# Three moving operands of a sliding-window attention and gated feed-forward kernel are stored in reverse and read with a step of minus one

## Chip, cores and metric

The kernel runs on one core of one Trainium2 chip, in one launch. The time is device microseconds of that core, the median of several executions: 691.52 us before (three runs, 691.29 to 691.58). In the profile PE is the matmul engine and PEld its weight loads, DVE the vector engine, ACT the scalar engine, POOL the general one, SP the engine that issues most DMAs.

## What is computed

Attention over 4 batches x 8 heads, 768 positions, head size 64; each position sees a window of 128 positions and 4 sink positions. Then a feed-forward layer on 3072 tokens, 512 to 2048 to 512, with the gate `h - tanh(h)`:

```python
scores = scale * np.matmul(q, k.transpose(0, 1, 3, 2))
scores = np.where(is_sink | in_window, scores, -1000000000.0)
a = softmax(scores)                       # over keys
attn_out = np.matmul(a, v)
x = attn_out.transpose(0, 2, 1, 3).reshape(B * S, H * D)
h = x @ w_in
out = (h - np.tanh(h)) @ w_out
```

All data are float32 but for the feed-forward weights, which arrive as 64-bit words and are decoded on DVE.

## The kernel before

The work is cut into 12 chunks of 256 positions (`CH`), each with four units of two heads. Per unit: scores (`products`, L484 or L491), a mask and row maximum on DVE (L503, L509), exponentials on ACT (L517), normalisation (L538, L543), transposes of the probabilities on PE (L570), and masked copies of them into `pts` (L577, L584). Per chunk or pair of units, `attend` multiplies by the values (L618 for the sinks, L624 for the window) and leaves x, transposed, in PSUM.

Most matmuls are **split**: a float32 operand is written as a high part, rounded to the type `float32r`, and a low part that is the rest. A product takes two or three matmuls over such parts, in place of one plain float32 matmul. An operand's high part is written by an ACT copy and its low part by a DVE subtraction:

- keys of a unit: `ks`, one row of 392 keys for each of two heads, high and low parts in the two halves of the partitions (L448, L453). The first twelve units use plain float32 scores (L484) straight from the loaded keys and don't have `ks`; the other 36 take L491, four matmuls of 260 columns for each of the two 128-query tiles
- x of a chunk: `xh` and `xl`, 4 rows of 256 positions (L636, L640)
- weights: eight groups g for each of the two weight matrices k. `wt[k, g]` holds high and low part (L671, L676). For k = 0 (first weights) it is viewed as 4 rows of 256, for k = 1 (second weights) as 2 rows of 512

A step n of the feed-forward layer treats one chunk and one group. `mm1` (L695): 24 matmuls of 256 columns into `hps`, where the first weights are the stationary operand and xh or xl the **moving** one. `gate`: tanh on ACT (L700), a difference on DVE (L703), high part gh on ACT (L707), low part gl on DVE (L711). `mm2` (L743): 12 matmuls of 512 columns into `ops`, where gh or gl is stationary and the second weights are **moving**. There are 96 steps, so 2304 matmuls at L695 and 1152 at L743. After a chunk's last group the sums are copied (L754) and stored.

All engines' programs are written in an order that a planner works out beforehand: every piece of work is added with an engine, a duration, a due time and the tiles that it reads and writes, and `order` simulates the engines and picks the due piece that can start. The score matmuls, the transposes and the products with the values are placed among the feed-forward matmuls in that way. The durations and due times are constants in the code.

Of the kernel before, what the change touches and what calls it, by code (L numbers as in the profile page):

```python
# [9 lines left out]
F32 = mybir.dt.float32  # L10
F32R = mybir.dt.float32r
# [3 lines left out]
ALU = mybir.AluOpType  # L15
# [3 lines left out]
P = 128  # L19
DM = H * D  # L20
DFF = 2048
NPAIR = H // 2
# [4 lines left out]
KW = WIN + TS  # L27
KPACK = P + NT * TS
CH = 2 * P
# [123 lines left out]
def _words(t):  # L153

    w = t.rearrange("p (n w) -> p n w", w=2)
    return w[:, :, 0], w[:, :, 1]


def _decode_part(nc, m, lo, hi, i):


    if i == 0:
        nc.vector.tensor_scalar(m, hi, 3, 0x3FFFFFF8, op0=ALU.logical_shift_left, op1=ALU.bitwise_and)
    elif i == 1:
        nc.vector.scalar_tensor_tensor(m, lo, 29, m, op0=ALU.logical_shift_right, op1=ALU.bitwise_or)  # L165
    else:
        nc.vector.scalar_tensor_tensor(m, hi, 0xC0000000, m, op0=ALU.bitwise_and, op1=ALU.bitwise_or)  # L167


def _decode(nc, m, t):  # L170
    lo, hi = (w.bitcast(U32) for w in _words(t))
    for i in range(3):
        _decode_part(nc, m.bitcast(U32), lo, hi, i)


class Work:
# [63 lines left out]
def _banded(tc, qd, kp, vp, vs, masks, w_in, w_out, ident, pts, early, out):  # L240
    nc = tc.nc
    et = mybir.EngineType
    with ExitStack() as ctx:
# [193 lines left out]
        qh, ql, ks, pr, st, xps, xh, xl, sps, tps = ({} for _ in range(10))  # L437

        def split(u):

            def k_high(h):
                if h == 0:
                    t = hpool.tile([P, NPAIR * CH], F32R, tag="ha", name=f"ks{u}")
                    ks[u] = t[:, : 2 * KW].rearrange("p (h k) -> p h k", h=2)
                r = slice(64 * h, 64 * h + 64)
                nc.scalar.copy(ks[u][r, h, :], kt[u][r, :])  # L448

            def k_low(h):  # L450
                k, t = ks[u], kt[u]
                r, o = slice(64 * h, 64 * h + 64), slice(64 * (1 - h), 64 * (1 - h) + 64)
                nc.vector.tensor_tensor(k[o, h, :], t[r, :], k[r, h, :].bitcast(F32), op=ALU.subtract)  # L453

            def q_high():
                t = hpool.tile([P, 2, 2, CH], F32R, tag="hb", name=f"q{u}")
                qh[u], ql[u] = t[:, 0], t[:, 1]
                nc.scalar.copy(qh[u], qt[u])  # L458

            def q_low():  # L460
                nc.vector.tensor_tensor(ql[u], qt[u], qh[u].bitcast(F32), op=ALU.subtract)

            t = due_unit(u) - 5000
            k, q = ([s] for s in slots(u))
            old = [("x", 2)] + [("xu", 2, i) for i in range(NPAIR)] if u == 3 * NPAIR else []
            work.add("ACT", 525, t, q_high, q, ["qh"] + old)
            work.add("DVE", 705, t, q_low, q + ["qh"], ["ql"], port=True)
            for h in range(2):
                work.add("ACT", 425, t, lambda h=h: k_high(h), k, [("ks", h)] + old)
                work.add("DVE", 590, t, lambda h=h: k_low(h), k, [("ks", h)], port=True)  # L470
# [122 lines left out]
        def attend(cc, p0, pairs):  # L593

            b, c = chunks[cc]
            key, banks = (cc, p0), range(pairs // 2)

            def sink_rows():
                xps[key] = [ps_x.tile([P, 2, CH], F32, tag="x", name=f"x{cc}_{p0}")]
                for t in range(2):  # L600
                    nc.tensor.transpose(  # L601
                        xps[key][0][:, 1, t * P : (t + 1) * P],
                        zt[:, t].bitcast(F32).rearrange("p n a b c -> p (n a b c)"), ident,
                    )

            def sink_copy(m):

                nc.scalar.activation(zr[:, m, :], xps[key][0][:, 1, :], AF.Copy, scale=odd[:, m : m + 1])

            def values():  # L610
                if pairs == NPAIR:
                    ps = ps_t.tile([P, 2, 2, P], F32, tag="t", name=f"x{cc}_2")
                    xps[key].append(ps.rearrange("p a b q -> p a (b q)"))
                plan = [(2 * c, 0, CH, 1), (2 * c + 1, P, CH, 3)]
                if c > 0:
                    plan.append((2 * c - 1, 0, P, 0))
                for i in banks:
                    nc.tensor.matmul(xps[key][i], lhsT=vsink[:, p0 // 2 + i], rhs=zr, start=True, stop=False)  # L618
                for p in range(p0, p0 + pairs):
                    for n, (i, a, z, blk) in enumerate(plan):  # L620
                        for h in range(2):
                            rhs = pts[:, place(NPAIR * cc + p), h].rearrange("p a b -> p (a b)")[:, blk * P : blk * P + z - a]
                            hd = (2 * p + h) * D
                            nc.tensor.matmul(  # L624
                                xps[key][(p - p0) // 2][h * 64 : h * 64 + 64, p % 2, a:z],
                                lhsT=vt[cc, i][:, hd : hd + D], rhs=rhs,
                                start=False, stop=p % 2 == 1 and n == len(plan) - 1,
                            )

            def x_high(i):  # L630
                if p0 == 0 and i == 0:
                    where, a, b = (hpool, "hb", "ha") if home(cc) == 2 else (xpool, "xh", "xl")
                    xh[cc] = where.tile([P, NPAIR, CH], F32R, tag=a, name=f"xh{cc}")
                    xl[cc] = where.tile([P, NPAIR, CH], F32R, tag=b, name=f"xl{cc}")
                r = slice(p0 + 2 * i, p0 + 2 * i + 2)
                nc.scalar.copy(xh[cc][:, r, :], xps[key][i])  # L636

            def x_low(i):
                r = slice(p0 + 2 * i, p0 + 2 * i + 2)
                nc.vector.tensor_tensor(xl[cc][:, r, :], xps[key][i], xh[cc][:, r, :].bitcast(F32), op=ALU.subtract)  # L640

            last = NPAIR * cc + p0 + pairs - 1
            d = due_unit(last) + 5500
            work.add("PE", 230, d + 1500, sink_rows, [("z", i) for i in range(NPAIR)], ["x"])
            for m in range(2):
                work.add("ACT", 270, d + 2000, lambda m=m: sink_copy(m), ["x"], [("zr", m)])
            v = [vslot[cc, i] for i in range(max(0, 2 * c - 1), 2 * c + 2)]
            pt = [(f"pt {k}", place(NPAIR * cc + i)) for k in ("whole", "own", "before") for i in range(p0, p0 + pairs)]
            need = pt + ["vsink", ("zr", 0), ("zr", 1)] + v
            work.add("PE", (340 + 735 * pairs if c == 0 else 200 + TK * pairs), d + 3500, values, need, ["x", "t"][: pairs // 2])  # L650
            for i in banks:
                x = [("xu", home(cc), p0 + 2 * i), ("xu", home(cc), p0 + 2 * i + 1)]
                work.add("ACT", 490, d + 5000, lambda i=i: x_high(i), ["xt"[i]], x + [("x", home(cc))] * (p0 + i == 0))
                work.add("DVE", 690, d + 5200, lambda i=i: x_low(i), ["xt"[i]], x)


        wm, wt = {}, {}

        def weights(k, g):
            key, r = (k, g), count[0] % 2  # L660
            count[0] += 1

            wm[key] = pts[:, 2 + r].rearrange("p h a b -> p (h a b)")

            def bits(i):
                lo, hi = (w.bitcast(U32) for w in _words(wraw[key]))
                _decode_part(nc, wm[key].bitcast(U32), lo, hi, i)

            def high():
                t = wpool.tile([P, 2, WG], F32R, tag=f"w{k}_{g}", name=f"w{k}_{g}")  # L670
                nc.scalar.copy(t[:, 0, :], wm[key])  # L671
                wt[key] = t.rearrange("p a (d f) -> p a d f", d=(NPAIR, 2)[k])

            def low():
                t = wt[key].rearrange("p a d f -> p a (d f)")
                nc.vector.tensor_tensor(t[:, 1, :], wm[key], t[:, 0, :].bitcast(F32), op=ALU.subtract)  # L676

            d = due_group(g) + WNEXT * k - WLEAD
            for i in range(3):
                work.add("DVE", (684, 1224, 1224)[i], d, lambda i=i: bits(i), [("wr", k, g, 0), ("wr", k, g, 1)], [("dw", r)], port=True)  # L680
            work.add("ACT", 985, d + 1000, high, [("dw", r)], [("w", *key)])
            work.add("DVE", 1224, d + 1500, low, [("dw", r)], [("w", *key)], port=True)
# [147 lines left out]
        for n in range(NS):  # L830
            cc, g = order[n]
            first_half(n)
            gate(n)
            if n:
                second_half(n - 1)
                cc, g = order[n - 1]
# [212 lines left out]
```

## Time and profile before

| | |
|---|---|
| median of the runs | 691.52 us |
| span of the profiled execution | 689.9 us |
| PE busy / PEld busy | 98% / 87% |
| DVE busy / ACT busy | 62% / 53% |
| PE's share of the chain that ended last | 90% |
| mean granted clock of PE | 0.999 |
| HBM read / written | 44.96 / 6.29 MB |

The profiled execution's span runs from its first to its last instruction; the timed runs hold some 1.6 us more. In the rows of groups, the numbers behind the bar are busy time in us, mean duration of one in ns, then the idle time of the engine just before them and what ended it. Durations of matmuls contain their latency, and matmuls overlap, so the spacing of a run of them says more than the duration of one.

### The profile page before, as it was taken

How to read it: one execution, taken by the hardware profiler on the slowest of the kernel's cores; microseconds unless marked ns; L12 is line 12 of the kernel's file. 1: busy time of each engine (PE TensorE's matmuls, PEld its weight loads, DVE VectorE, ACT ScalarE, POOL GpSimd, SP SyncE). 2: the span in 40 equal slices, each digit the busy share in tenths (PEclk: the TensorE clock that was granted, in tenths of full speed). 3: DMA queues.
4: the chain of work that ended last, by engine and by line, in shares of the span. 5: the costliest groups of instructions: out<-in, count | busy, mean ns of one | idle time of the engine just before them, and what ended most of it. 6: DMA issues, size and time to landing. Idle time of an engine off the chain costs nothing.

```text
span 689.9 us, 12423 instructions
## 1 busy us (share of the span) xinstructions
PE 677.0 (98%) x4604; PEld 599.9 (87%) x4604; DVE 427.5 (62%) x1084; ACT 367.0 (53%) x1001; POOL 52.0 (8%) x201
## 2 busy tenths in 40 slices
PE   7999999999999999999999999999999999999996
PEld 5777899999889889889988988998898898988985
DVE  7889999847755747556646665565564755663221
ACT  5996433347655646456555655555465545644222
POOL 6220010000000010000001000001000000000000
PEclk9999999999999999999999999999999999999999
DMA  6789800022130121112113112112112212100001
GB/s 205 241 273 384 314 1 5 1 88 55 55 89 28 43 92 55 28 49 84 39 28 109 55 27 90 29 53 85 32 42 75 55 28 61 55 1 1 31 1 35
DMA packets 31713, 52.14 MB, mean 76 GB/s; under 512 B 3228, under 2 KB 21020, under 8 KB 31644
## 3 DMA queue, kind: packets, MB, share of 16 engines
q1 hardware_dynamic: 31340, 50.93, 23.3%
q8 instruction: 38, 0.62, 0.4%
q10 hardware_dynamic: 304, 0.33, 0.2%
q14 instruction: 31, 0.25, 0.1%
HBM read 44.96 MB, written 6.29 MB: 74 GB/s over the span
## 4 chain that ended last, share of the span: by engine, by line
PE 90%; DVE 3%; ACT 3%; SPq 1%; issue 1%; POOL 1%; DMA 0%; POOLq 0%; DVEq 0%; ACTq 0%
PE o L743 39%; PE h L695 38%; PE s L491 5%; PE x L624 5%; PE t L570 2%; ACT p L543 1%; ACT p L517 1%; PE x L618 1%; DVE pt L584 1%; DVE pt L167 1%; DMA qk<-kp 0%; DVE p L509 0%; DVE pt L165 0%; PE x L601 0%; SPq L104 0%
## 5 line engine op out<-in xcount | busy, mean ns | idle before, releaser
L695 PE MATMUL h<-xh,w 128*128 128x256 f32 x1536 | 286.9, 280 | 0.0
L695 PEld LDWEIGHTS h<-xh,w 128*128 128x128 f32 x1536 | 241.1, 188 | 1.9 <-issue 0.2
L695 PE MATMUL h<-xl,w 128*128 128x256 f32 x768 | 214.6, 279 | 0.0
L743 PE MATMUL o<-w,gh 128*128 128x512 f32 x768 | 199.5, 400 | 0.7 <-ACT gh L707 0.6
L743 PEld LDWEIGHTS o<-w,gh 128*128 128x128 f32 x768 | 137.5, 188 | 28.9 <-ACT gh L707 1.5
L695 PEld LDWEIGHTS h<-xl,w 128*128 128x128 f32 x768 | 144.2, 188 | 1.7
L743 PE MATMUL o<-w,gl 128*128 128x512 f32 x384 | 106.8, 398 | 0.0
L700 ACT ACTIVATE graw<-h 128x512 f32<-128x512 f32 x96 | 57.0, 594 | 91.1 <-PE h L695 91.0
L517 ACT ACTIVATE p<-p,st 128x132 f32<-128x132 f32 x192 | 76.1, 398 | 52.6 <-DVE st L509 51.7
L711 DVE TENSOR_TENSOR gl<-h,gh 128x512 fp32r<-128x512 f32 x96 | 66.1, 688 | 48.7 <-ACT gh L707 48.5
L703 DVE TENSOR_TENSOR h<-h,graw 128x512 f32<-128x512 f32 x96 | 66.4, 692 | 44.9 <-ACT graw L700 44.2
L743 PEld LDWEIGHTS o<-w,gl 128*128 128x128 f32 x384 | 70.8, 188 | 16.9 <-issue 1.0
L707 ACT CAST gh<-h 128x512 fp32r<-128x512 f32 x96 | 55.6, 579 | 49.6 <-DVE h L703 49.5
L503 DVE COPY_PREDICATED s<-above,s 128x256 f32<-128x256 uint32 x80 | 34.0, 425 | 75.3 <-PE s L491 74.7
L543 ACT ACTIVATE p<-p,st 128x132 f32<-128x132 f32 x192 | 62.0, 396 | 5.7 <-DVE st L538 5.3
L509 DVE CUSTOM_DVE_ANT_0 p<-s,mask 128x132 f32<-128x132 f32 x192 | 49.0, 292 | 8.2 <-POOL qraw L342 2.1
L548 POOL CAST z<-p 128x16 fp32r<-128x16 f32 x48 | 10.2, 213 | 499.9 <-ACT p L543 498.0
L458 ACT CAST q<-qraw 128x512 fp32r<-128x512 f32 x36 | 22.4, 622 | 45.9 <-PE s L491 43.9
L491 PE MATMUL s<-ks,q 128*128 128x260 f32 x288 | 46.3, 283 | 0.0
L491 PEld LDWEIGHTS s<-ks,q 128*128 128x128 f32 x288 | 42.5, 188 | 4.2
L640 DVE TENSOR_TENSOR xl<-x,xh 128x512 fp32r<-128x512 f32 x24 | 16.5, 689 | 44.9 <-ACT xh L636 44.9
L453 DVE TENSOR_TENSOR ks<-kraw,ks 64x392 fp32r<-64x392 f32 x72 | 40.4, 561 | 2.2
(80 smaller groups left out, 573.8 us busy)
## 6 DMA issues: line engine op xcount, KB each, us to landing
qraw<-qd SPq DMA_DIRECT2D x36, 256.0 KB, 2.7
wraw<-w_in SPq DMA_DIRECT2D x16, 512.0 KB, 8.2
wraw<-w_out SPq DMA_DIRECT2D x16, 512.0 KB, 10.5
kraw<-kp SPq DMA_DIRECT2D x37, 196.0 KB, 2.6
v<-vp SPq DMA_DIRECT2D x27, 256.0 KB, 2.9
out<-ob SPq DMA_DIRECT2D x24, 256.0 KB, 2.2
qk<-kp SPq DMA_DIRECT2D x8, 196.0 KB, 5.1
qk<-qd SPq DMA_DIRECT2D x16, 64.0 KB, 4.9
```

The costliest lines, as they stand in the source:

```text
L453: nc.vector.tensor_tensor(k[o, h, :], t[r, :], k[r, h, :].bitcast(F32), op=ALU.subtract)
L491: nc.tensor.matmul(ps[h][:, :WIN], lhsT=q[:, h, t * P : (t + 1) * P], rhs=rhs, start=i == 0, stop=i == 1,)
L509: nc.vector.tensor_tensor_reduce(out=pr[u][:, j, :], in0=ps[h][:, P:WIN], in1=mask[:, kind, :], scale=-0.125, scalar=BIG, op0=ALU.add, op1 ...
L517: nc.scalar.activation(e, e, AF.Exp, bias=st[u][:, j : j + 1], scale=-1.0, accum_out=st[u][:, 4 + j : 5 + j],)
L543: nc.scalar.activation(pr[u][:, j, :], pr[u][:, j, :], AF.Copy, scale=s[:, 8 + j : 9 + j])
L624: nc.tensor.matmul(xps[key][(p - p0) // 2][h * 64 : h * 64 + 64, p % 2, a:z], lhsT=vt[cc, i][:, hd : hd + D], rhs=rhs, start=False, stop=p ...
L695: nc.tensor.matmul(hps[n][:, f, :], lhsT=w, rhs=x, start=r == 0, stop=r == 11)
L700: nc.scalar.activation(gr[n], hps[n], AF.Tanh)
L703: nc.vector.tensor_tensor(hps[n], hps[n], gr[n], op=ALU.subtract)
L707: nc.scalar.copy(gh[n], hps[n])
L711: nc.vector.tensor_tensor(gl[n], hps[n], gh[n].bitcast(F32), op=ALU.subtract)
L743: nc.tensor.matmul(ops[cc, t], lhsT=(gh, gh, gl)[i][n][:, f, t * P : (t + 1) * P], rhs=wt[1, g][:, (0, 1, 0)[i], f, :], start=first and no ...
```

## The change

The tiles for `ks`, `xh`, `xl` and the second weights keep their size and place, but are handled through a view with the innermost dimension reversed (`[..., ::-1]`). What is written through the view lands last element first, and a matmul that takes its moving operand from the view reads descending addresses, with a step of minus one element, and meets the elements in their old logical order. The results keep their place and order. The first weights, the stationary operands, the plain float32 keys, the transposed probabilities and the values stay as they were. The weight copies are given as rows (`_rows`) so that the second weights can be reversed row by row, and the low parts of the second weights are computed from operands of that shape.

```diff
+def _rows(k, t):
+    return t.rearrange("p (d f) -> p d f", d=(NPAIR, 2)[k])
...
-                    ks[u] = t[:, : 2 * KW].rearrange("p (h k) -> p h k", h=2)
+                    ks[u] = t[:, : 2 * KW].rearrange("p (h k) -> p h k", h=2)[:, :, ::-1]
...
-                    xh[cc] = where.tile([P, NPAIR, CH], F32R, tag=a, name=f"xh{cc}")
-                    xl[cc] = where.tile([P, NPAIR, CH], F32R, tag=b, name=f"xl{cc}")
+                    xh[cc] = where.tile([P, NPAIR, CH], F32R, tag=a, name=f"xh{cc}")[:, :, ::-1]
+                    xl[cc] = where.tile([P, NPAIR, CH], F32R, tag=b, name=f"xl{cc}")[:, :, ::-1]
...
                 t = wpool.tile([P, 2, WG], F32R, tag=f"w{k}_{g}", name=f"w{k}_{g}")
-                nc.scalar.copy(t[:, 0, :], wm[key])
                 wt[key] = t.rearrange("p a (d f) -> p a d f", d=(NPAIR, 2)[k])
+                if k:
+                    wt[key] = wt[key][:, :, :, ::-1]
+                nc.scalar.copy(wt[key][:, 0], _rows(k, wm[key]))
...
-                t = wt[key].rearrange("p a d f -> p a (d f)")
-                nc.vector.tensor_tensor(t[:, 1, :], wm[key], t[:, 0, :].bitcast(F32), op=ALU.subtract)
+                t = wt[key]
+                nc.vector.tensor_tensor(t[:, 1], _rows(k, wm[key]), t[:, 0].bitcast(F32), op=ALU.subtract)
```

## The prediction

> **What bounds the kernel now.** I read the page first (shares, then the chain that ended last), then the chain in order of time, the timeline of the matmul engine, the groups of instructions with shapes kept apart, and the list of waits.
>
> ```profile
> span 689.9 us, 12423 instructions
> PE 677.0 (98%) x4604; PEld 599.9 (87%) x4604; DVE 427.5 (62%) x1084; ACT 367.0 (53%) x1001; POOL 52.0 (8%) x201
> PEclk9999999999999999999999999999999999999999
> PE 90%; DVE 3%; ACT 3%; SPq 1%; issue 1%; POOL 1%; DMA 0%; POOLq 0%; DVEq 0%; ACTq 0%
> PE o L743 39%; PE h L695 38%; PE s L491 5%; PE x L624 5%; PE t L570 2%; ACT p L543 1%; ACT p L517 1%; PE x L618 1%; DVE pt L584 1%; DVE pt L167 1%; DMA qk<-kp 0%; DVE p L509 0%; DVE pt L165 0%; PE x L601 0%; SPq L104 0%
> ```
>
> The profiled execution's span is 689.9 us; the median of the runs, 691.52, is 1.6 us more, for what lies around the span. Sums below are made against the span and the 1.6 put back. The matmul engine is 98% busy at a full granted clock and holds 90% of the chain. Three lines make 82% of the chain: L743 (39%), L695 (38%) and L491 (5%). These are exactly the lines whose moving operands the change turns round. So the question is what one matmul of each costs while the stream runs, and whether that cost has anything to do with the order of addresses.
>
> A matmul's duration in the groups contains its latency, so it is not the price of one more. The price is the step from one to the next, and the chain in order of time gives it (start, length, how many):
>
> ```profile
> 42.94 1.75 PE s L484 x8
> ...
> 273.26 0.47 PE s L491 x4
> 273.74 0.44 PE t L570 x4
> 274.17 5.61 PE o L743 x24
> 279.78 0.48 PE s L491 x4
> 280.26 5.65 PE h L695 x48
> ```
>
> L695 (256 columns): 5.65 / 48 = 117.7 ns. L743 (512 columns): 5.61 / 24 = 233.75 ns. L491 (260 columns): two pieces of 4, 0.95 / 8 = 118.75 ns. Between the first two, 256 more columns cost 116.05 ns: **0.4533 ns a column**, with 1.7 ns fixed. Plain fp32 streams stand beside them: L484 (260 columns) steps 1.75 / 8 = 218.75 ns, and the transposes of L570 (128 columns):
>
> ```profile
> 328.65 0.60 PE L570 MATMUL t<-ident,p 128*128 128x128 f32 x4
> L570 PE MATMUL t<-ident,p 128*128 128x128 f32 x192 | 29.3, 274 | 2.5 <-DVE pt L584 1.3 <-ACT p L543 0.8 <-ACT pt L577 0.4
> ```
>
> Four of them last 0.60 us and one alone 274 ns, so the step is (600 - 274) / 3 = 108.7 ns. From 128 to 260 columns the plain stream costs (218.75 - 108.7) / 132 = 0.834 ns a column and 2.0 ns fixed. Half of that is 0.417. If plain fp32 takes two passes over its columns, which the rows suggest and don't prove, one pass could cost 0.417 ns a column, and the split matmuls pay 0.036 ns a column, 9%, above it. Does the weight load cause that excess? Every matmul has one load of the same size:
>
> ```profile
> L695 PEld LDWEIGHTS h<-xh,w 128*128 128x128 f32 x1536 | 241.1, 188 | 1.9 <-issue 0.2
> L743 PEld LDWEIGHTS o<-w,gh 128*128 128x128 f32 x768 | 137.5, 188 | 28.9 <-ACT gh L707 1.5 <-issue 0.5 <-ACT graw L700 0.2
> ```
>
> L743 loads half as many weights per column as L695, yet the excess is 18.2 ns a matmul there (233.75 against 512 x 0.417 + 2.0 = 215.5) and 9.0 ns at L695 (117.7 against 108.7): it goes with the moving columns, not with the loads. So there is an excess in reading 4-byte moving elements, and the change touches that reading. That is why a gain can't be shut out. Nothing in this trace reads a moving operand in another direction or with another step, so no row prices a step of minus one.
>
> **The change part by part.** *What moves:* nothing. The sequence of instructions on each engine stays, as do the number of matmuls, columns, weight loads and DMAs. Two kinds of instruction get another shape: the casts and subtractions that write xh and xl go from one run of 512 elements to two of 256, and those of the eight second weight groups from 1024 to two of 512. No wait is added.
>
> *The writers.* 24 + 24 instructions on x, 8 + 8 of the 16 + 16 on weights, 72 + 72 on keys write descending addresses (the subtractions on x and the weights also read one descending input):
>
> ```profile
> L636 ACT CAST xh<-x 128x512 fp32r<-128x512 f32 x24 | 14.1, 586 | 34.1 <-PE x L624 34.1
> L640 DVE TENSOR_TENSOR xl<-x,xh 128x512 fp32r<-128x512 f32 x24 | 16.5, 689 | 44.9 <-ACT xh L636 44.9
> L671 ACT CAST w<-pt 128x1024 fp32r<-128x1024 f32 x16 | 16.8, 1051 | 4.1 <-DVE pt L167 4.1
> L676 DVE TENSOR_TENSOR w<-pt,w 128x1024 fp32r<-128x1024 f32 x16 | 19.5, 1222 | 0.7 <-ACT w L671 0.7
> L448 ACT CAST ks<-kraw 64x392 fp32r<-64x392 f32 x72 | 37.2, 517 | 0.9
> L453 DVE TENSOR_TENSOR ks<-kraw,ks 64x392 fp32r<-64x392 f32 x72 | 40.4, 561 | 2.2
> L584 DVE TENSOR_TENSOR pt<-t,below 128x512 f32<-128x512 f32 x32 | 22.0, 687 | 10.1 <-PE t L570 9.6
> ```
>
> From 512 to 1024 elements DVE's price grows by (1222 - 689) / 512 = 1.04 ns an element, one at a time, and L584, which writes four runs of 128, costs 687 ns like one run of 512. So runs are free, and an engine that writes element by element should not mind the direction: **0** for each. Upper end: each takes twice as long, on ACT 14.1 + 8.4 + 37.2 = 59.7 us and on DVE 16.5 + 9.8 + 40.4 = 66.7 us. Lower end: 0, since the same elements pass one at a time. What hides even the upper end is the idle time of both engines (53% and 62% busy) and the lead of the work over its user. For the keys of one unit:
>
> ```profile
> 202.25 0.56 DVE L453 TENSOR_TENSOR ks<-kraw,ks 64x392 fp32r<-64x392 f32 x1
> 208.42 0.65 PE L491 MATMUL s<-ks,q 128*128 128x260 f32 x4
> ```
>
> The last key subtraction ends at 202.81 and its matmuls start at 208.42: 5.6 us of lead against 2 x (0.52 + 0.56) = 2.2 us of doubling for the two heads. Where that cover is missing is the start-up, where the chain itself passes through xl:
>
> ```profile
> 24.48 0.60 DVE xl L640
> 41.10 0.59 DVE xl L640
> 58.03 0.60 DVE xl L640
> ```
>
> There a doubling would cost 3 x (0.59 + 0.69) = 3.8 us. So the writers are worth 0, at most about +4 us.
>
> *The readers*, which decide: 1536 + 768 = 2304 matmuls of L695, 768 + 384 = 1152 of L743, 288 of L491.
>
> ```profile
> L695 PE MATMUL h<-xh,w 128*128 128x256 f32 x1536 | 286.9, 280 | 0.0
> L695 PE MATMUL h<-xl,w 128*128 128x256 f32 x768 | 214.6, 279 | 0.0
> L743 PE MATMUL o<-w,gh 128*128 128x512 f32 x768 | 199.5, 400 | 0.7 <-ACT gh L707 0.6
> L743 PE MATMUL o<-w,gl 128*128 128x512 f32 x384 | 106.8, 398 | 0.0
> L491 PE MATMUL s<-ks,q 128*128 128x260 f32 x288 | 46.3, 283 | 0.0
> ```
>
> The lower end is the whole excess gone: 2304 x 9.0 + 1152 x 18.2 + 288 x (118.75 - 110.4) = 20.7 + 21.0 + 2.4 = **-44 us**. The upper end is the nearest row with a slower stream, the plain fp32 step of 0.834 ns a column: L695 at 215.5 ns (+97.8), L743 at 429.0 (+195.3), L491 at 218.75 (+100): 225 + 225 + 29 = **+479 us**. Between ends so far apart I take the row it is nearest to, the same matmul on the same bytes in ascending order: **0**. A descending run of 256 or 512 elements covers the same addresses as before, each once, next to its neighbour. L491 starts its 260 columns at four different offsets in its tile and still steps 118.75 ns where the line through L695 and L743 gives 1.7 + 260 x 0.4533 = 119.5, so the price follows the count of columns and no particular start.
>
> The Trainium skill, "SBUF — State Buffer", section "Door 1: The DMA port swizzle", says that the memory is read in 16-byte lines, that two hits in a line are needed for full rate and that each change of line pays a penalty. By it, four fp32 elements share a line in either direction and the sum stays 0; no run here shows the line itself.
>
> Sum: 0 for what moves, 0 for the writers, 0 for the readers: 689.9 + 1.6 = **691.5 us**.
>
> **The rivals.**
>
> *The excess goes (faster).* If the extra 0.036 ns a column belongs to ascending reads, for instance because the next element comes late when the addresses climb, descending ones run at 0.417. For it: the excess is real, follows the moving columns and is missing in the plain streams. Against it: nothing ties it to a direction. Its full price is 44 us, but the early stretch may not pass it on:
>
> ```profile
> 31.00:138.00 107.00, 104.41 (x693) 91.15 (x692) 99.49 (x174) 56.87 (x140) 10.83 (x29) 1.00 0.46 163
> 138.00:300.00 162.00, 161.98 (x1119) 146.02 (x1118) 98.05 (x261) 92.05 (x250) 8.82 (x39) 1.00 0.20 60
> ```
>
> From 31 to 138 us DVE (third pair) is busy 99.5 of 107 us decoding weights, so matmuls that finish earlier there would wait for it; later it is busy 98 of 162. With 384 of L695 and 169 of L743 in that stretch, 3.5 + 3.1 = 6.5 us are in doubt:
>
> ```profile
> 31.00:138.00 107.00, 48.16 (x384) 46.94 (x384) 1.00 0.46 163
> 31.00:138.00 107.00, 42.49 (x169) 30.69 (x170) 1.00 0.46 163
> ```
>
> That gives 647 to 654 us, and anything between that and 691 for a part. The Trainium skill, "TensorE: Matmul & The Clock Gate", section "Wait — 56ns, not 53.3ns?", gives N / 2.4 + 2.5 ns for a back-to-back matmul, 109.2 for 256 columns and 215.8 for 512. The trace disagrees for the split matmuls (117.7 and 233.75); if the change restored that rule, an estimate by the page is 43 us gained.
>
> *Descending reads are fetched singly (slower).* The stream takes an element each 0.453 ns, and if it keeps that up only by fetching neighbours together in ascending order, a step of minus one falls to the plain stream's 0.834. Place: every matmul of the three lines. Price: +479 us, 1170 us in all; it decides as soon as a column costs over 0.453. A milder form, in which the present excess doubles, costs +44 and gives 735. For it: the stream is already above its pass, so it has no slack to hide a slower fetch. Against it: the same elements lie together in either direction.
>
> *The change does nothing it says.* If the step were undone when the operands are laid out, the time would be the forecast's; it is in that chance.
>
> *The writers double (slower).* Worth up to 4 us, 695; it needs an element-wise engine to mind direction.
>
> What the matmul engine waited for shows why the rest can be left out:
>
> ```profile
> PE t L570 <- ACT p L543: 0.8, 1, 0.8
> PE s L484 <- DVE st L509: 0.7, 3, 0.3
> PE o L743 <- ACT gh L707: 0.6, 2, 0.3
> ```
>
> These follow the longest in its list, 1.3 us of L570 for L584. L743's own entry is 0.6 us for gh; L695 and L491 have none, so none of the three lines waits for x, for second weights or for keys.
>
> **How the numbers follow.** A measurement of this kernel tells about 0.2% (1.4 us) from no change. Forecast, no change: 0.42, with 690.1 to 692.9 as its own range. Faster by the excess, whole or in part: 0.33; it is high because the excess lies in just the reading that changes, and a row for the direction is missing. Slower: 0.25, of which 0.10 up to a doubled excess (the writers among them) and 0.15 beyond, up to the plain rate. Range: from 647 (whole excess, early stretch too) to 736 (excess doubled): 0.42 + 0.33 + 0.10 = 0.85; the bound at 1170 is left out.
>
> **What would show it.** In the changed trace the chain's pieces of L695 x48, L743 x24 and L491 x4 should again last 5.65, 5.61 and 0.47 us. Lasting 5.2 and 5.2 they show the first rival; 10.3 the second. Casts of L636 and subtractions of L640 at 586 and 689 ns show the writers free; at 1000 ns or more, not. The forecast is wrong if one column of a split matmul costs anything but 0.453 ns. A gain at the matmuls that the span doesn't show would be found as new waits of L743 for gh (L707) or of L695 for weights in the stretch up to 138 us.

## The result and the profile after

The changed kernel takes 696.79 us against 691.41 in the same comparison: a ratio of 1.0074, 95% interval 1.006 to 1.0088. It is **slower by 5.4 us**, where no change was forecast. The figure lies outside the 690.1 to 692.9 us that the forecast of no change gave itself; it is only within the wide range, in the part to which the prediction gave a chance of 0.10.

The page of the changed kernel, the same rows as before:

```profile
span 695.1 us, 12423 instructions
PE 681.6 (98%) x4604; PEld 604.6 (87%) x4604; DVE 428.3 (62%) x1084; ACT 367.5 (53%) x1001; POOL 52.3 (8%) x201
```

The span grew by 5.2 us and PE's busy time by 4.6; DVE and ACT stayed within 0.8. So the time is in the matmul stream. The chain in order of time of the changed kernel (start, length, how many) says which matmul; h at L701 was L695, o at L749 was L743, s at L495 was L491:

```profile
276.07 5.60 PE o L749 x24
281.67 0.48 PE s L495 x4
282.15 5.76 PE h L701 x48
```

The second product and the key scores kept their pieces (5.60 for 5.61 us, 0.48 for 0.47 and 0.48). **The first product's piece went from 5.65 to 5.76 us**: 120.0 ns a matmul for 117.7. Over 2304 matmuls that is 2304 x 2.3 = 5.3 us, about the whole loss. The writers, in the groups of the changed kernel, cost what they did:

```profile
L640 ACT CAST xh<-x 128x512 fp32r<-128x512 f32 x24 | 14.1, 587 | 34.2 <-PE x L628 34.1
L644 DVE TENSOR_TENSOR xl<-x,xh 128x512 fp32r<-128x512 f32 x24 | 16.5, 689 | 45.1 <-ACT xh L640 45.1
L682 DVE TENSOR_TENSOR w<-pt,w 128x1024 fp32r<-128x1024 f32 x16 | 19.5, 1221 | 0.7 <-ACT w L678 0.7
```

One more thing stood in the trace of before and had been missed. Between 95 and 140 us the chain alternates between the second chunk and the third, whose x lies in another pool. Of before:

```profile
118.42 2.83 PE h L695 x24
124.05 2.73 PE h L695 x24
```

and of after:

```profile
119.10 2.87 PE h L701 x24
124.77 2.83 PE h L701 x24
```

The third chunk steps at 2.73 / 24 = 113.8 ns, the second at 117.9, in one kernel, with the same shapes and types. After the change they are at 117.9 and 119.6. One difference between the two is where their tiles lie: the program's allocation puts the third chunk's x at byte 0 modulo 512 in each partition, all others' at 384, and all weights at 320. So a matmul's price is more than its count of columns. That the place makes this difference was a guess, which the runs bear out in part only, and the question became whether the loss is the direction or the place.

### The profile page after: what moved, and what is told of

It is laid out like the page before. It is cut to its first block, busy times and chain, and to the rows that moved or that the text cites. A ratio compares the mean times of both kernels' runs of the same rounds, so it can differ in the third digit from the quotient of the medians.

```text
span 695.1 us, 12423 instructions
## 1 busy us (share of the span) xinstructions
PE 681.6 (98%) x4604; PEld 604.6 (87%) x4604; DVE 428.3 (62%) x1084; ACT 367.5 (53%) x1001; POOL 52.3 (8%) x201
## 4 chain that ended last, share of the span: by engine, by line
PE 90%; DVE 3%; ACT 3%; SPq 1%; issue 1%; POOL 1%; DMA 0%; POOLq 0%; ACTq 0%
PE o L749 38%; PE h L701 38%; PE s L495 5%; PE x L628 5%; PE t L574 2%; ACT p L547 1%; ACT p L521 1%; PE x L622 1%; DVE pt L588 1%; DVE pt L167 1%; DMA qk<-kp 0%; DVE p L513 0%; DVE pt L165 0%; PE x L605 0%; SPq L104 0%
## 5 line engine op out<-in xcount | busy, mean ns | idle before, releaser
L701 PE MATMUL h<-xh,w 128*128 128x256 f32 x1536 | 292.1, 283 | 0.0
L701 PEld LDWEIGHTS h<-xh,w 128*128 128x128 f32 x1536 | 242.6, 188 | 1.9 <-issue 0.2
L701 PE MATMUL h<-xl,w 128*128 128x256 f32 x768 | 216.4, 282 | 0.0
L749 PE MATMUL o<-w,gh 128*128 128x512 f32 x768 | 199.8, 402 | 0.4 <-ACT gh L713 0.3
L749 PEld LDWEIGHTS o<-w,gh 128*128 128x128 f32 x768 | 137.9, 188 | 28.4 <-ACT gh L713 1.1
L701 PEld LDWEIGHTS h<-xl,w 128*128 128x128 f32 x768 | 144.3, 188 | 1.7
L749 PE MATMUL o<-w,gl 128*128 128x512 f32 x384 | 107.2, 401 | 0.0
L749 PEld LDWEIGHTS o<-w,gl 128*128 128x128 f32 x384 | 70.8, 188 | 16.8 <-issue 1.0
L495 PEld LDWEIGHTS s<-ks,q 128*128 128x128 f32 x288 | 42.6, 188 | 4.4
L495 PE MATMUL s<-ks,q 128*128 128x260 f32 x288 | 46.2, 283 | 0.0
```

The source lines that it names most:

```text
L495: nc.tensor.matmul(ps[h][:, :WIN], lhsT=q[:, h, t * P : (t + 1) * P], rhs=rhs, start=i == 0, stop=i == 1,)
L701: nc.tensor.matmul(hps[n][:, f, :], lhsT=w, rhs=x, start=r == 0, stop=r == 11)
L749: nc.tensor.matmul(ops[cc, t], lhsT=(gh, gh, gl)[i][n][:, f, t * P : (t + 1) * P], rhs=wt[1, g][:, (0, 1, 0)[i], f, :], start=first and no ...
```

## The experiments

All times below stand beside runs of the kernel before on the same chip. *Distance* is the start of the moving run's lowest byte minus that of the stationary operand, modulo 256 bytes: 64 for x in the kernel before, 192 for the third chunk.

### x back in ascending order

```diff
-                    xh[cc] = where.tile([P, NPAIR, CH], F32R, tag=a, name=f"xh{cc}")[:, :, ::-1]
-                    xl[cc] = where.tile([P, NPAIR, CH], F32R, tag=b, name=f"xl{cc}")[:, :, ::-1]
+                    xh[cc] = where.tile([P, NPAIR, CH], F32R, tag=a, name=f"xh{cc}")
+                    xl[cc] = where.tile([P, NPAIR, CH], F32R, tag=b, name=f"xl{cc}")
```

> xh and xl back in ascending order; second weights and split keys stay reversed. After the change a matmul of the first feed-forward product (256 columns of x) follows the one before it by 120.0 ns where it was 117.8, and 2304 x 2.2 ns = 5.1 us is the whole loss; the second product stayed at 233.4 ns. If the loss belongs to x alone: about 691.5 us, with the second product at 233.4 ns and the key scores within 1 ns of 119. If reversing costs something on every operand, or in the writers: 693 us or more.

Measured: 691.72 us against 691.93, ratio 0.9997 (0.9987 to 1.0006). Reversed second weights and keys cost nothing, on balance, that can be measured; the loss is x's alone. The trace holds one thing more. All pieces of the second chunk between 95 and 140 us took 2.83 us in the kernel before; here, with x at the same place and ascending as there, they alternate between two prices, and so do the third chunk's:

```profile
107.75 2.73 PE h L701 x24
...
118.80 2.82 PE h L701 x24
```

Both pieces are the second chunk's. The only difference from the kernel before is the reversal of the other operands, so the price of an ascending x isn't settled by its own place and direction.

### Moving the x tiles, without and with the reversal

In the kernel before and in the changed one, the pool of x is allocated ahead of two others. x then lies at 0 modulo 512, distance 192 as in the third chunk:

```diff
-        pp, sm = pool("pp", 2), pool("sm", 4)
-        xpool, gpool = pool("xpool", 2), pool("gpool", 2)
+        xpool = pool("xpool", 2)
+        pp, sm, gpool = pool("pp", 2), pool("sm", 4), pool("gpool", 2)
```

> The kernel before, nothing reversed; the pool of xh and xl is allocated ahead of two others, so that the tiles start at 0 modulo 512 bytes in a partition, not at 384. Nothing else is changed in what is computed. In the trace of before the third chunk, whose x lies in another pool at 0 modulo 512, steps at 113.8 ns, all others at 117.8. Theory of place (where the moving run lies, against the weights or absolutely, sets its step): all chunks step at about 113.8, 2112 x 4.0 ns = 8.5 us gained, about 683 us. Rival, the third chunk is quicker for what goes on around it (early work, other engines): 117.8 stays, 691.5 us.

> The changed kernel with the same move of the x tiles to 0 modulo 512. In the trace of after the third chunk steps at 117.8 ns, the others at 120.0. Theory of place: all chunks at 117.8, about 692 us, so reversing costs 4 ns at this place against 2.2 ns at the old one. Rival, a descending run has a price of its own that doesn't depend on place: 120.0 stays, 697 us.

Measured: 687.31 us ascending (ratio 0.9932, 0.9916 to 0.9949) and 693.50 reversed (1.0021, 1.0011 to 1.003). The theory of place holds in kind: x ascending gains from another place, with nothing else changed, and a reversed x falls to 117.7 ns there. In size it holds in part: 4.6 us of the 8.5 forecast. The chain of the ascending run shows why, since chunks step at two speeds, the eleventh of twelve still as the third did and the last not:

```profile
606.47 5.46 PE h L695 x48
...
635.21 5.66 PE h L695 x48
```

That is 113.8 and 117.9 ns at one place. The place alone doesn't fix the price. Nor does it explain the pair that raised the question: the second chunk's x now lies where the third's does, modulo 512, and they still take 2.83 and 2.74 us, where the kernel before had 2.83 and 2.73:

```profile
118.54 2.83 PE h L695 x24
...
124.17 2.74 PE h L695 x24
```

The gain is in other chunks. Reversing cost 693.50 - 687.31 = 6.2 us at this place. The reversed run is 1.6 us above the kernel before although its pieces are equal; summed from the start of each matmul to the next, steps over 300 ns left out, h takes 271.4 us for 270.4 before and o 255.3 for 254.8, so most of it lies in the same two lines. The third chunk, quicker than 117.7 ns in the kernel before and not here, makes 0.7 us of it (192 x 3.9 ns).

### Places by themselves

A kernel that only multiplies: rows of 48 matmuls of 256 columns, in the three-term pattern of the first product, for each place and both directions.

```python
def up(b, n=256):
    return lambda s, d: x[:, s, b + d * 256 : b + d * 256 + n]
def down(b, n=256):
    return lambda s, d: x[:, s, b + d * 256 : b + d * 256 + n][:, ::-1]
...
for wo in (80, 0):                    # weights at 320, then 0 modulo 512 bytes
    for i in range(8):                # x in steps of 64 bytes, letters a to h
        for kind, move in (("up", up), ("dn", down)):
            ps = run(kind + ("", "z")[wo == 0] + "abcdefgh"[i], move(16 * i), wup(wo))
```

> Computes none of the reference: rows of 48 matmuls of 256 columns in the three-term pattern of the first product, high and low x against high and low weights, with nothing else running. Each row has another start of the x run, 0 to 448 modulo 512 bytes in steps of 64 (letters a to h), ascending (up) and descending (dn), first with the weights at 320 modulo 512 (as in the kernel), then at 0 (z). Theory of place, relative: the step depends on x minus weights, so the second half shows the pattern of the first shifted by five letters; ascending g at 320 gives 117.8, a gives 113.8, descending g 120.0, a 117.8. Absolute: both halves show the same pattern. Direction alone: all ascending rows alike, all descending rows alike and slower. If the other engines' traffic makes the excess, all rows fall to about 109.

Its chain in order of time, one piece a row of the sweep (distances: a, e and zd 192, f and ze 0, g and zf 64):

```profile
21.51 5.65 PE upa L65 x48
...
67.11 5.47 PE upe L65 x48
72.58 5.65 PE dne L65 x48
78.23 5.74 PE upf L65 x48
83.97 5.68 PE dnf L65 x48
89.65 5.65 PE upg L65 x48
95.31 5.75 PE dng L65 x48
...
146.79 5.46 PE upzd L65 x48
152.26 5.65 PE dnzd L65 x48
157.91 5.74 PE upze L65 x48
163.66 5.68 PE dnze L65 x48
169.34 5.65 PE upzf L65 x48
174.99 5.75 PE dnzf L65 x48
```

With nothing else running, the kernel's place gives the kernel's prices: 5.65 us ascending and 5.75 reversed (g), and 5.47 against 5.65 at the third chunk's (e). So other engines' traffic isn't the cause. When the weights move by 320 bytes the pattern moves along: equal distances give equal prices, so it is the *difference* of the two places modulo 256 that counts, not either alone. Ascending rows run from 5.46 to 5.75, descending ones from 5.65 to 5.76. At distance 0 (f) reversing even gains 0.06 us: a reversal has no single price, it costs or saves by place, though no descending row went below 5.65. Letter a, at distance 192 like e, gave 5.65 ascending, the other of the two states seen above.

> Computes none of the reference: rows of matmuls as in the run of places, nothing else running, the weights at 320 modulo 512 bytes. Letters a to p are starts of x in steps of 16 bytes over 256 bytes, from 192 behind the weights' start modulo 256 (a) by e = 0, i = 64 (the kernel's place), m = 128. The run of places gave up a 113.9, e 119.6, i 117.8, m 118.5 and dn a 117.7, e 118.3, i 119.8, m 120.0. Theory, the moving reads collide with the reads of the next weight load, and the place sets how: rows of half (weight loads of 64 columns, not 128, the same moving run) lose about half of the excess over 108.7 ns or more, and their places and directions differ less. Rival, the moving run alone has the excess (its own start in a line or a bank): half rows equal the full ones. Wide rows (512 columns for each load of 128): the collision theory has the same or a smaller spread in ns per matmul, 4 to 6 ns around 233; the rival has twice the spread. Rows named again hold place a ascending after 24 matmuls at e, i, m, i, e: if the state depends on what ran before, they fall on 113 or 118; if not, all 113.9. Single 16-byte steps: if only 64-byte steps matter, letters of one group of four are alike.

The finer sweep repeated the prices and added three facts. Its chain:

```profile
203.72 2.86 PE toge L65 x24
206.59 5.46 PE again L65 x48
212.04 2.83 PE togi L65 x24
214.87 5.45 PE again L65 x48
220.32 2.85 PE togm L65 x24
223.17 5.65 PE again L65 x48
...
245.42 5.59 PE up_wide_a L65 x24
251.01 5.46 PE up_wide_e L65 x24
...
267.57 5.60 PE dn_wide_a L65 x24
273.17 5.60 PE dn_wide_e L65 x24
...
295.69 5.44 PE up_half_e L65 x48
...
329.35 5.76 PE dn_half_m L65 x48
```

Place a ascending takes 5.45 us after a stretch at i and 5.65 after one at m: its price depends on what ran before. The distance of the stretch before doesn't settle it: after one at e, distance 0, it took 5.46, and as the first row behind the warm-up, which is at distance 0 too, 5.65. A descending row at distance 192 has two prices as well: 5.65 for dne, 5.76 for dna of this sweep (at 112.09). Rows of 512 columns ascending run from 227.5 ns (e) to 233.0 (a), descending ones at 233.3 wherever they lie; the second product of the kernel lies at a, the slow end, and so had nothing to lose by reversal. And weight loads of 64 columns in place of 128 left prices of 5.44 to 5.76: the theory that the excess is the bytes of the weight loads colliding with the moving reads expected it to shrink by half, and that **fell**; only the pattern over places shifted. The theory's other forecast came out: it gave rows of 512 columns a spread over the places of 4 to 6 ns a matmul, where its rival gave twice the spread of 256 columns, and they spread by 5.5 (227.5 to 233.0), rows of 256 by 5.8 (113.8 to 119.6). So what the place adds comes once with a matmul, whatever its columns, and didn't shrink with the weight load. Why the distance counts stays open.

### Which order costs

Rows with the order of elements taken apart into groups of four (16 bytes): `line` reads groups last to first with ascending elements inside, `in` reads groups in order with elements inside last to first, `two` and `twodn` take every second element.

> Computes none of the reference: rows of 48 matmuls as before, at places a, e, i, m, l (16-byte steps behind 192 modulo 256 from the weights). Which part of a descending run costs? line: groups of four elements (16 bytes) in descending order, elements within a group ascending. in: groups ascending, elements within a group descending. If it is the order of the groups, line rows look like dn rows (117.7 to 120 at every place) and in rows like up rows (113 to 120 by place); if it is the order of the elements, the reverse. two and twodn: every second element, so twice the span of memory for 256 columns: if the excess comes with each 16 bytes fetched, it doubles, about 126 to 131; if it comes with each column, they equal up and dn. c and b: 192 and 128 columns: if the step follows 0.453 ns a column, 88.7 and 59.7; if a weight load has a floor, the b rows stop near 109, the c rows too.

```profile
44.54 5.47 PE up_l L65 x48
...
72.85 5.75 PE dn_l L65 x48
...
101.45 5.75 PE line_l L65 x48
...
129.95 5.47 PE in_l L65 x48
...
146.47 10.88 PE two_e L65 x48
...
190.16 11.20 PE twodn_a L65 x48
...
251.50 5.36 PE up_c_e L65 x48
...
294.36 5.36 PE up_b_e L65 x48
```

`line` repeats `dn` and `in` repeats `up` at all five places. So what costs is the order of the 16-byte groups, not a step of minus one; groups of another size were not tried. Every second element takes 10.88 / 48 = 226.7 ns (233.3 descending), what 512 columns side by side take (227.5, 233.3). Neither forecast, 126 to 131 or no change, had that: the price goes with the stretch of memory passed over, 64 or 128 groups, not with the columns. That is 113.3 / 64 = 1.77 ns a group at best and 120.0 / 64 = 1.88 at worst. And 192 and 128 columns both take 5.36 / 48 = 111.7 ns: there something that comes with each matmul, not with its columns, sets the step. Each loads 128 columns of weights, so that load may be it; no run with fewer weights and as few columns shows it.

In the kernel, with x alone in each of the two orders:

```diff
-                    xh[cc] = where.tile([P, NPAIR, CH], F32R, tag=a, name=f"xh{cc}")
+                    xh[cc] = where.tile([P, NPAIR, CH], F32R, tag=a, name=f"xh{cc}").rearrange("p n (c e) -> p n c e", e=4)[:, :, :, ::-1]
...
-            x = (xh, xl, xh)[t][cc][:, d, :]
+            x = (xh, xl, xh)[t][cc][:, d]
```

and `[:, :, ::-1, :]` for groups that descend.

> The kernel before with only x in another order: groups of four elements (16 bytes) ascend, the four elements within a group are read last first. Alone, such rows equalled ascending ones at all five places. If the order of the groups makes the loss: first product at 117.8 ns, about 691.6 us, although every step within a group is minus one. If any step of minus one costs, or the writers do: 120 ns and 697 us.

> The kernel before with only x in another order: groups of four elements descend, the four within a group are read in ascending order. If the order of the groups makes the loss: first product at 120.0 ns, about 697 us, the whole loss of the change from x alone, although no step within a group is negative. If a step of minus one between elements makes it: 691.6 us.

Measured: 691.65 us (ratio 1.0001, 0.9991 to 1.001) for elements reversed inside ascending groups, and 696.31 (1.0067, 1.005 to 1.0084) for descending groups with ascending elements. Their chains:

```profile
280.31 5.66 PE h L698 x48
```

```profile
281.99 5.76 PE h L698 x48
```

The first has steps of minus one inside each group and loses nothing; the second, without any, loses 4.7 us, most of the change's 5.4.

### Better places

The kernel before, nothing reversed, with x at distance 192 and the halves gh, gl moved too, so that the second product lies at distance 0 (e), and the changed kernel likewise:

```diff
-        pp, sm = pool("pp", 2), pool("sm", 4)
-        xpool, gpool = pool("xpool", 2), pool("gpool", 2)
+        xpool = pool("xpool", 2)
+        pool("gap", 1).tile([P, 16], F32, tag="gap", name="gap")
+        gpool, pp, sm = pool("gpool", 2), pool("pp", 2), pool("sm", 4)
```

> The kernel before, nothing reversed, x at 0 modulo 512 as in the run with x moved, and gh, gl moved to 64 modulo 256, the place of the second weights. In the rows of 512 columns this place (e) stepped at 227.5 ns and the place of before (a) at 233.0. Theory of place: 1152 x 5.8 ns = 6.7 us below the run with x moved, about 680.6 us, the second product's step near 227.5. If places found with nothing else running don't carry over to the kernel: 687 us.

> The changed kernel with the same two moves. In the rows of 512 columns a descending run stepped at 233.3 to 233.5 ns at every place. Theory, a descending run is slow wherever it lies: second product stays at 233.4, first at 117.8, about 693.5 us as with x moved alone, so reversing costs some 13 us against the same places in ascending order. If place gives to descending runs what it gives to ascending ones: 687 us.

Measured: 686.54 us (ratio 0.9923, 0.9907 to 0.994) and, reversed, 693.29 (1.0023, 1.0013 to 1.0032). The first is far from the 680.6 us that its theory of place gave and near the 687 of the rival; the second is as forecast. Ascending, the second product reached its place's price, but the first fell back in most of its pieces:

```profile
575.76 3.62 PE x L625 x48
581.00 5.46 PE h L696 x48
599.91 5.46 PE o L744 x24
605.84 5.65 PE h L696 x48
```

Behind the products with the values (x) the first product takes 5.46 us here, behind a stretch of the second (o) at its new place 5.65: again what ran before has a part. It is no rule: in the last chunk it stays at 117.8 ns (5.30 us for 45, at 634.74) behind products with the values and eight matmuls of o. Reversed, the second product stayed at 5.60 us for 24 and the first at 5.66: what these places give to ascending runs, descending ones don't get.

Without the gap, gh and gl at 0 and the second product at distance 64 (i):

```diff
-        pp, sm = pool("pp", 2), pool("sm", 4)
         xpool, gpool = pool("xpool", 2), pool("gpool", 2)
+        pp, sm = pool("pp", 2), pool("sm", 4)
```

> The kernel before, nothing reversed, x at 0 and gh, gl at 0 modulo 256, so that the second product's moving weights lie 64 behind its stationary operand (place i, 229.6 ns alone in rows of 512 columns). With x at place a the first product took 113.9 in most steps when the second product stood at 233, and 116.7 to 117.8 when it stood at 227. If the first product's state follows from what runs before it: between those, second product 229.6, first 114 to 118, 683 to 689 us. If the two products are independent: first product as in the run with x moved, about 683.5 us.

Measured: 683.16 us, ratio **0.9874 (0.9858 to 0.9891)**, the fastest version here and faster than both kernels. Both accounts had allowed for this time (683 to 689 and 683.5 us), so it doesn't decide between them. Its chain has both prices at once:

```profile
596.71 5.51 PE o L743 x24
602.69 5.46 PE h L695 x48
```

Last, the second product at distance 0 again and x at distance 32, for a state that doesn't flip:

```diff
+        pool("gap", 1).tile([P, 16], F32, tag="gap", name="gap")
+        gpool = pool("gpool", 2)
+        pool("gap2", 1).tile([P, 8], F32, tag="gap2", name="gap2")
+        xpool, pp, sm = pool("xpool", 2), pool("pp", 2), pool("sm", 4)
```

> The kernel before, nothing reversed, gh, gl at 64 modulo 256 as in the run with both moved (second product 227.5), x at 96 modulo 256, 32 behind the weights (place g, 116.7 ns alone, one state only in the rows so far). If rows found alone carry over: 2304 x 0.5 ns = about 1 us below the run with both moved, 685.5 us; if the state after the second product is another: up to 692 us.

Measured: 686.36 us (ratio 0.992, 0.9904 to 0.9937), with 5.47 us for 24 of o and 5.61 for 48 of h (116.9 ns, as alone). It behaves as the rows said and is worth no more than the run with both moved. Of x at distance 112 (letter l), which alone took 5.44 to 5.47 us, no kernel was tried.

## Why the prediction was wrong, by its own steps

**What bounds the kernel: right.** The three lines and their steps carried the time; all of the loss came as a longer step of one of them.

**Nothing moves, no wait is added, the writers cost 0: right.** Their rows are the same within 1 ns, runs and descending addresses included.

**The readers cost 0: wrong, and it is the step that failed.** It had been taken from "the same matmul on the same bytes in ascending order". That price is not the matmul's: it goes with its place and with what ran before, 113.3 to 120 ns over the places tried, and turning the order of the groups round gives another figure of that band (120.0 at the kernel's place). The 5.4 us are those of x at L695, 2304 x 2.3 = 5.3 by its step, and with x alone put back nothing of the loss was left (ratio 0.9997). That the order of the groups makes it is shown; by what mechanism it does is open. For L743 and L491 the 0 was right, for L743 because its place was already as slow ascending (233.0) as descending (233.3).

**Two arguments behind that 0 fell.** "The price follows the count of columns and no particular start" rested on L491's four starts, whose average doesn't show what each start costs; the third chunk's 2.73 against 2.83 us, for the same columns, stood in the same trace and spoke against it. And the straight line of 0.4533 ns a column with 1.7 ns fixed came out of two prices that belong to two places. With it falls, in part, the reading that the excess goes with the moving columns: what the place adds, some 6 ns, comes once with a matmul. The prediction also cited the Trainium skill, "SBUF — State Buffer", section "Door 1: The DMA port swizzle": memory is read in 16-byte lines, and two hits in a line are needed for full rate. The runs agree that groups of 16 bytes matter, but neither their direction nor the place is in that rule, and they disagree with the two hits: at two elements a group the matmul took 226.7 ns, twice its best price at four.

**The first rival (the excess goes, 647 to 654 us): wrong in its end.** It took 108.7 ns as what 256 columns could cost. The rows of 128 and 192 columns of this type stop at 111.7, and the best row of 256 gives 113.3. It was right that the excess lies in reading the moving operand, and a part of it can be had, by place and not by direction: 683.16 us.

**The second rival (slower): right in its sign, and at one of its three lines; wrong in its price and mechanism.** The plain stream's rate would have been 1170 us, a doubled excess 735. The stream goes on at its rate; each matmul of x takes 2.3 ns more, a quarter of the 9.0 ns that the doubling assumed. Whether elements are fetched singly in descending order is answered too: elements reversed within their groups cost nothing.

**The check offered at the end** (5.65, 5.61 and 0.47 us again) worked as meant: the one piece that moved, 5.65 to 5.76, is the loss.

## What to carry to other kernels

When matmuls run back to back for the whole span, read the step of each kind from the chain, chunk by chunk, and not from an average: two chunks with the same shapes and different steps showed, before the change was made, that the price isn't fixed by the columns. For a moving operand of `float32r`, read its 16-byte groups in ascending order, and treat the place of the moving run against the stationary one, modulo 256 bytes, as something to be tuned: the order in which pools are allocated was worth 1.3% here. Measure the choice in the kernel itself, since the gain at one place depends on what ran just before.

## What the runs showed of the hardware that wasn't expected

- With nothing else running, matmuls of the same shape and type took 113.9 ns at distance 192, 117.7 at 64 and 119.6 at 0 (rows e, g, f); the pattern follows the distance between moving and stationary operand and repeats after 256 bytes (rows e to g against zd to zf).
- One place has two prices, 113.5 and 117.7 ns, and the matmuls before have a part in which it is (5.45 us after i, 5.65 after m).
- The price of a moving run of this type goes by the memory that it passes, in the order of 16-byte groups: every second element of 512 costs 226.7 ns for 256 columns, and groups last to first cost up to 120.0 ns where elements last to first inside them cost nothing.
- In rows of this type, each matmul with its load of 128 columns of weights, 128 and 192 columns both took 111.7 ns, where 256 took 113.3 at best.
